# Attention and two MLPs on one core: the second block of queries is taken from the second batch

## The chip, the cores and the metric

The kernel runs on one core of one Trainium2 chip. The metric is the device time of one execution in microseconds (us); lower is better. TensorE is called PE in the profile (its weight loads PEld), VectorE DVE, ScalarE ACT, GpSimd POOL and SyncE SP.

## The reference

A causal attention with a forget gate (4 batches, 8 heads, 576 positions, head size 64) is followed by two MLPs over its 2304 rows of 512 numbers. Everything is float32.

```
scores = q @ k.T / 8 + min(-(cum_i - cum_j), 0)      # cum: running sum of max(s, 0) along the positions
attn   = softmax(causal(scores)) ;  x = attn @ v      # then (batch, position) x (head, size) -> 2304 x 512
h      = x @ w_in1 ;  x2  = (s * relu(h)**2 + b) @ w_out1
h      = x2 @ w_in2;  out = (max(h, 0) + alpha * min(h, 0)) @ w_out2
```

The MLPs treat each row by itself, so the order in which rows go through them is free as long as each result goes to its row of the output.

## The kernel before, in words

**Units of attention.** Work is cut into 32 units. A unit is one batch, one pair of heads and one of two ranges of queries: range 0 is queries 0 to 319, which see keys 0 to 319; range 1 is queries 320 to 575, which see all 576 keys. The list `units` (L210) goes batch by batch, within a batch range by range, within a range over the four pairs. Four units with the same batch and range are called a group here. Per head, range 0 has three blocks of queries (64, 128 and 128 rows that see 64, 192 and 320 keys) and range 1 has two (128 rows each that see 448 and 576 keys).

**A unit's steps.** `load_qk` (L257), `load_v` (L268) and `load_cum` (L283) issue its DMAs on SP's queue. `transpose_qk` (L302) turns q and k with DVE. `scores` (L337), once per head, prepares the gate term on DVE (L362) and the causal mask on POOL (L366, after memsets at L345, L358 and L360), multiplies q and k on PE (L384, or L386 and L387), adds and finds the maximum on DVE (L388), takes exp on ACT (L394) and scales on POOL (L403). `values` (L409), once per head, transposes the probabilities on PE (L434), copies them out of PSUM, multiplies by v (L450) and writes the result into `x_block(t)`, the input tile of MLP block t (L455 to L467).

**Native and split units.** Units 0 to 7 (`NATIVE = 2 * NP`, L54) are native: PE multiplies the float32 tiles as they are, and a listing of PE shows two passes for each product. From unit 8 on each operand is split into a high and a low float32r part (ACT, POOL and DVE work at L106, L107, L326 to L334), and scores and values are each two float32r products; `values` then copies and adds at L465 and L466 in place of the one copy at L463.

**MLP blocks and pace.** The rows are cut into 9 blocks of 256 (T), in the order in which the units produce them, and go through the first MLP block by block while attention runs on, then through the second. A block has 16 steps f, each with `up` (PE at L575; ACT and DVE at L596 to L599; a split at L106 and L107) and `down` (PE at L616, in the second MLP L626), and at its end `finish` (L631), which copies the result out (L637, L639) and stores it. In block 0 of the first MLP each step also converts one packet of weights (`load_packet`, L157: DMA of 1 MB, ACT at L116, DVE at L117 and L118, then a split on ACT and POOL). `reached(t)` (L656) says how many units must be done before block t can be read, and `pace` (L660) how many units are emitted at each step. For t = 0 to 8 it gives 4, 8, 12, 16, 20, 24, 28, 28 and 32 units.

**Order.** The program is emitted in the order of the loop at L679; a planner then orders each engine's instructions by its own estimates and by what is ready. So each engine's list mixes MLP steps, weight packets and attention at fine grain.

**Where the stages lie.** Unit 4, the first of the second group, has its scores on PE from 49.58 us on; DVE's last instruction on a packet of weights (L118) starts at 148.19 us; block 0 of the first MLP is copied out (L639) at 165.97 us and block 1 at 234.35 us. The units of a group follow each other without a gap.

Of the kernel before, what the change touches and what calls it, by code (L numbers as in the profile page):

```python
# [18 lines left out]
def tile_forget_attention__then__two_mlps(  # L19
# [20 lines left out]
    nc = tc.nc  # L40
    B, H, S, D = q.shape
    NT, DM = out.shape
    DFF = w_in1.shape[1] // 2
    P = 128
    NP = H // 2
    NCC = DM // P
    NF = DFF // P
    T = 256
# [3 lines left out]
    R1 = IB[2][1]  # L52
    QK = S - R1 + S
    EARLY, NATIVE = NP, 2 * NP  # L54

# [47 lines left out]
    def split(hi, lo, src, lo_eng=nc.vector):  # L105
        nc.scalar.copy(hi, src)  # L106
        lo_eng.tensor_tensor(out=lo, in0=src, in1=hi.bitcast(F32), op=ALU.subtract)  # L107
# [34 lines left out]
    for f in range(len(SPARE), NF):  # L142
        at = int((f - len(SPARE)) * PACE)
# [50 lines left out]
    def x_block(t):  # L194
        if t not in xf:
            xf[t] = xfp.tile([P, NCC, T], F32, tag="xf", name=f"xf{t}")
        return xf[t]
# [9 lines left out]

    units = [(b, pr, rng) for b in range(B) for rng in range(2) for pr in range(NP)]  # L210
    HALF = (slice(0, 64), slice(64, 128))
    early_bufs = list(range(4 * NF - 2, -1, -2)) + [4 * NF - 1]

# [195 lines left out]
    def values(u, h):  # L409

        own = HALF[h]
        q0, q1, nq = u.q0, u.q1, u.q1 - u.q0

        width = [q1 - max(q0, P * c) for c in range(5) if P * c < q1]
        last_c = len(width) - 1
        banks = ([(0, 0), (1, 320)], [(2, 64)]) if u.rng == 0 else ([(0, 0), (1, 256)], [(2, 0), (3, 256), (4, 448)])
        av = u.bank("av", f"av{h}")
        for n_bank, bank in enumerate(banks):  # L420
            f0, fn = bank[0][1], bank[-1][1] + width[bank[-1][0]]
            tp = u.bank("tr", f"pt{h}_{n_bank}")
            moves = []
            for c, off in bank:
                for r in u.blocks:
                    i0, i1 = IB[r]
                    if P * c >= i1:
                        continue

                    partial = r and P * c > i0  # L430
                    o = off + i0 - max(q0, P * c)
                    moves.append((not partial, -c if partial else o, o, r, min(P * c, S - P)))
            for _, _, o, r, k0 in sorted(moves):
                nc.tensor.transpose(tp[:, o : o + P], u.probs[h][r][:, k0 : k0 + P], ident)  # L434
            n_p = (2 * h + n_bank) % 2
            if u.native:
                pf = two.tile([P, 512], F32, tag=("ph", "pl")[n_p], name=f"pf_{u.tag}_{h}_{n_bank}")
                (nc.scalar.copy, nc.vector.tensor_copy)[n_p](pf[:, f0:fn], tp[:, f0:fn])
                parts = (pf,)
            else:  # L440
                ph = two.tile([P, 512], F32R, tag="ph", name=f"ph_{u.tag}_{h}_{n_bank}")
                pl = two.tile([P, 512], F32R, tag="pl", name=f"pl_{u.tag}_{h}_{n_bank}")
                split(ph[:, f0:fn], pl[:, f0:fn], tp[:, f0:fn])
                parts = (ph, pl)
            yield
            for z, part in enumerate(parts):
                for c, o in bank:
                    w = width[c]
                    lhs = (u.vn if u.native else u.vs[h])[:, c].rearrange("p z d -> p (z d)")
                    nc.tensor.matmul(  # L450
                        av[:, nq - w : nq], lhs, part[:, o : o + w],
                        start=(c == 0 and z == 0), stop=(c == last_c and z == len(parts) - 1),
                        skip_group_check=True,
                    )
        t0 = u.b * S + q0  # L455
        while t0 < u.b * S + q1:
            t = t0 // T
            t1 = min((t + 1) * T, u.b * S + q1)
            a = t0 - u.b * S - q0
            cols = slice(a, a + t1 - t0)  # L460
            dst, src = x_block(t)[own, u.pr, t0 - t * T : t1 - t * T], av[own, cols]
            if u.native:
                nc.scalar.copy(dst, src)  # L463
            else:
                nc.scalar.copy(dst, av[HALF[1 - h], cols])  # L465
                nc.vector.tensor_tensor(out=dst, in0=src, in1=dst, op=ALU.add)  # L466
            t0 = t1  # L467
        yield
# [12 lines left out]
    def attention():  # L481
# [22 lines left out]
        yield from alternate(transpose_qk(us[1]), scores(us[0], 0))  # L504
        yield from alternate(transpose_qk(us[2]), scores(us[0], 1))
        yield from alternate(transpose_qk(us[3]), scores(us[1], 0), values(us[0], 0))
        yield from alternate(scores(us[1], 1), values(us[0], 1))
        yield from alternate(scores(us[2], 0), values(us[1], 0))
        u = Unit(EARLY)
        load_qk(u), load_cum(u), load_v(u)  # L510
# [46 lines left out]
    def mlp_block(layer, t, x):  # L557
# [73 lines left out]
        def finish():  # L631
            both = one.tile([P, 1024], F32, tag="res", name=f"res{layer}_{t}")
            for m in range(2):
                cols = slice(m * 512, (m + 1) * 512)
                res = both[:, cols]
                if m % 2:
                    nc.scalar.mul(res, accs[:, cols], 1.0 / W_SCALE)  # L637
                else:
                    nc.vector.tensor_scalar(  # L639
                        out=res, in0=accs[:, cols], scalar1=1.0 / W_SCALE, scalar2=None, op0=ALU.mult  # L640
                    )
                if layer == 0:
                    nc.sync.dma_start(out=x2_d[t, :, cols], in_=res)
                else:
                    nc.sync.dma_start(out=out[t * T + m * P : t * T + (m + 1) * P, :], in_=res)

        return up, down, finish

# [5 lines left out]
        return packets[layer, f]  # L654

    def reached(t):  # L656
        b, rest = divmod(min((t + 1) * T, NT) - 1, S)
        return NP * (2 * b + (1 if rest < R1 else 2))

    def pace(t):  # L660

        t += LEAD / NF
        n = int(t)
        return reached(n) + (t - n) * (reached(min(n + 1, NB - 1)) - reached(n)) if n < NB else len(units)
# [8 lines left out]
    while done < reached(0):  # L673
        next(side)
# [4 lines left out]
    for n in range(2 * NB * NF):  # L679
# [11 lines left out]
        for j in range(NF):  # L691
            at = LAG[1] + int((j - len(SPARE)) * PACE) if j >= len(SPARE) else j * SPACING - FIRST
# [42 lines left out]
```

## Time and profile before

| | |
|---|---|
| time, median of 3 runs | 1091.94 us (1088.45 to 1092.47) |
| the profiled execution: its time, its span | 1088.58 us, 1086.8 us |
| PE busy, share of the span | 1045.6 us, 96% |
| DVE busy | 666.8 us, 61% |
| ACT busy | 644.4 us, 59% |
| POOL busy | 478.4 us, 44% |

The span is the time from the first to the last instruction; the execution takes 1.8 us more than its span. In the row of PE busy by slices of 27 us, the first slices are the only ones with low digits: `5899999999...`; the granted clock of PE in the same slices is `9699899999...`, in tenths of 2.4 GHz.

### The profile page before, as it was taken

Reading aid. Unit: us, or ns where it says so; the run is one execution under the profiler, and the core shown is the slowest. Engines: PE = TensorE matmul, PEld = TensorE weight load, DVE = VectorE, ACT = ScalarE, POOL = GpSimd, SP = SyncE. Lnnn points to the kernel's source line nnn. Section 1 sums busy time; section 2 is a strip of 40 time slices with the busy share of each in tenths; the row PEclk is TensorE's granted clock in tenths of the full one; section 3 lists DMA queues with packets and bytes.
Section 4 is the critical chain, followed back from the end, with each engine's and each line's share of the span. In section 5 each row is a group of like instructions: output and inputs, shape, how many; then the busy total and the mean of one; then the engine's idle time right before and its main releaser. Section 6 shows DMA issues by size and latency. Waiting matters only on the chain.

```text
span 1086.8 us, 21253 instructions
## 1 busy us (share of the span) xinstructions
PE 1045.6 (96%) x7429; PEld 969.9 (89%) x7429; DVE 666.8 (61%) x1612; ACT 644.4 (59%) x1719; POOL 478.4 (44%) x868
## 2 busy tenths in 40 slices
PE   5899999999999999999999999899999999999998
PEld 3677799999999999999998999789999999999997
DVE  7699878787688877787565167943333333333332
ACT  3686767777767877777565467643444434434332
POOL 6688877665766757666464267820000000000000
PEclk9699899999999999999999999999999999999999
DMA  6987433343232422233134064510100100000000
GB/s 145 236 234 221 136 70 81 80 99 56 50 81 65 109 50 60 67 78 81 34 104 141 12 204 155 175 40 1 40 20 20 40 1 20 2 20 20 2 20 20
DMA packets 170059, 83.85 MB, mean 77 GB/s; under 512 B 135456, under 2 KB 155936, under 8 KB 169952
## 3 DMA queue, kind: packets, MB, share of 16 engines
q1 hardware_dynamic: 168272, 81.94, 28.3%
q8 instruction: 58, 0.95, 0.4%
q10 hardware_dynamic: 1680, 0.57, 0.2%
q14 instruction: 49, 0.40, 0.1%
HBM read 72.96 MB, written 9.51 MB: 76 GB/s over the span
## 4 chain that ended last, share of the span: by engine, by line
PE 67%; DVE 14%; DMA 5%; issue 4%; ACT 4%; POOL 3%; SPq 2%; DVEq 0%; POOLq 0%; ACTq 0%
PE hp L575 29%; PE acc L626 18%; PE acc L616 12%; PE pt L434 3%; DVE probs L362 3%; PE av L450 3%; DMA wo<-in_moe_w_out_dram 2%; DVE probs L388 2%; DVE wt L117 2%; DVE wt L118 2%; SPq L263 1%; DVE r L599 1%; DVE xs L331 1%; PE sc L387 1%; PE sc L386 1%
## 5 line engine op out<-in xcount | busy, mean ns | idle before, releaser
L575 PE MATMUL hp<-xh,w 128*128 128x256 f32 x2304 | 467.5, 285 | 5.6 <-ACT r L596 2.9
L575 PEld LDWEIGHTS hp<-xh,w 128*128 128x128 f32 x2304 | 378.6, 191 | 13.5 <-ACT r L596 4.4
L575 PE MATMUL hp<-xl,w 128*128 128x256 f32 x1152 | 327.2, 284 | 0.0
L575 PEld LDWEIGHTS hp<-xl,w 128*128 128x128 f32 x1152 | 220.3, 191 | 6.3 <-POOL probs L358 0.7
L626 PE MATMUL acc<-w,ring 128*128 128x512 f32 x864 | 220.4, 393 | 1.2 <-POOL ring L107 0.8
L616 PE MATMUL acc<-gh,w 128*128 128x256 f32 x1024 | 201.9, 288 | 5.3 <-ACT gh L106 5.0
L604 DVE SCALAR_TENSOR_TENSOR ring<-ring,nalpha 128x256 f32<-128x256 f32 x144 | 74.6, 520 | 177.3 <-ACT ring L603 176.3
L626 PEld LDWEIGHTS acc<-w,ring 128*128 128x128 f32 x864 | 154.1, 189 | 28.1 <-POOL ring L107 1.2
L616 PEld LDWEIGHTS acc<-gh,w 128*128 128x128 f32 x1024 | 161.1, 191 | 10.7 <-ACT gh L106 7.4
L616 PE MATMUL acc<-gl,w 128*128 128x256 f32 x512 | 149.4, 292 | 2.8 <-POOL gl L107 2.7
L596 ACT ACTIVATE ring<-hp 128x256 f32<-128x256 f32 x144 | 55.5, 385 | 138.6 <-PE hp L575 138.4
L107 POOL TENSOR_TENSOR gl<-r,gh 128x256 fp32r<-128x256 f32 x128 | 99.9, 781 | 63.8 <-ACT gh L106 62.6
L403 POOL TENSOR_SCALAR probs<-probs,sm 64x64 f32<-64x64 f32 (+4 forms) x160 | 93.5, 597 | 61.0 <-DVE sm L400 57.9
L394 ACT ACTIVATE probs<-probs,nm 64x64 f32<-64x64 f32 (+4 forms) x160 | 90.0, 562 | 46.3 <-DVE nm L388 44.9
L599 DVE TENSOR_SCALAR r<-r,gate_s,gate_b 128x256 f32<-128x256 f32 x144 | 80.5, 559 | 58.0 <-ACT r L598 55.8
L106 ACT CAST ring<-ring 128x256 fp32r<-128x256 f32 x144 | 58.5, 407 | 77.3 <-DVE ring L604 65.7
L616 PEld LDWEIGHTS acc<-gl,w 128*128 128x128 f32 x512 | 97.7, 191 | 5.2 <-POOL gl L107 5.1
L107 POOL TENSOR_TENSOR w<-wt,w 128x512 fp32r<-128x512 f32 x63 | 90.4, 1441 | 26.2 <-ACT w L106 22.1
L107 DVE TENSOR_TENSOR ring<-ring,ring 128x256 fp32r<-128x256 f32 x128 | 54.4, 425 | 61.1 <-ACT ring L106 61.1
L434 PE MATMUL pt<-ident,probs 128*128 128x128 f32 x480 | 79.8, 285 | 8.4 <-POOL probs L403 7.8
L388 DVE CUSTOM_DVE_ANT_0 probs<-sc,probs 128x320 f32<-128x320 f32 (+3 forms) x160 | 67.9, 427 | 23.9 <-PE sc L387 18.4
L596 ACT ACTIVATE r<-hp 128x256 f32<-128x256 f32 x144 | 54.6, 379 | 39.3 <-PE hp L575 33.2
(86 smaller groups left out, 1637.2 us busy)
## 6 DMA issues: line engine op xcount, KB each, us to landing
wi<-in_moe_w_in_dram SPq DMA_DIRECT2D x32, 512.0 KB, 4.5
wo<-in_moe_w_out_dram SPq DMA_DIRECT2D x32, 512.0 KB, 5.0
cum<-cum_d SPq DMA_DIRECT2D x32, 288.0 KB, 3.5
cum<-cum_d SPq DMA_DIRECT2D x30, 160.0 KB, 3.1
nat<-in_k_dram SPq DMA_DIRECT2D x64, 72.0 KB, 2.3
x_d<-res SPq DMA_DIRECT2D x18, 256.0 KB, 2.4
x<-x_d SPq DMA_DIRECT2D x9, 512.0 KB, 4.3
out_dram<-res SPq DMA_DIRECT2D x18, 256.0 KB, 2.0
```

Of the source, the lines that this page charges most:

```text
L106: nc.scalar.copy(hi, src)
L107: lo_eng.tensor_tensor(out=lo, in0=src, in1=hi.bitcast(F32), op=ALU.subtract)
L388: nc.vector.tensor_tensor_reduce(out=pt[:rows, j0:j1], in0=scr, in1=pt[:rows, j0:j1], scale=-SCALE, scalar=init, op0=ALU.add, op1=ALU.min, ...
L394: nc.scalar.activation(pt[:rows, :n], pt[:rows, :n], AF.Exp, bias=nm[:rows, m : m + 1], scale=-1.0, accum_out=sm[:rows, m : m + 1],)
L403: nc.gpsimd.tensor_scalar(out=probs[r][:rows, :n], in0=probs[r][:rows, :n], scalar1=sm[:rows, m : m + 1], scalar2=1.0, op0=ALU.mult, op1=A ...
L434: nc.tensor.transpose(tp[:, o : o + P], u.probs[h][r][:, k0 : k0 + P], ident)
L575: nc.tensor.matmul(hs, a[:, c], b[:, c], start=(n == 0), stop=(n == len(terms) * NCC - 1))
L596: nc.scalar.activation(r, hs, AF.Relu, scale=1.0 / W_SCALE)
L599: nc.vector.tensor_scalar(out=r, in0=r, scalar1=gate_s[:, 0:1], scalar2=gate_b[:, 0:1], op0=ALU.mult, op1=ALU.add)
L604: nc.vector.scalar_tensor_tensor(out=r, in0=u, scalar=nalpha[:, f : f + 1], in1=r, op0=ALU.mult, op1=ALU.add)
L616: nc.tensor.matmul(acc[:, d], a[:, d * P : (d + 1) * P], b, start=(f == 0 and d % 2 == 0 and n == 0), stop=(f == NF - 1), skip_group_check ...
L626: nc.tensor.matmul(accs[:, m * DM : (m + 1) * DM], a[:, m * P : (m + 1) * P], b, start=(f == 0 and b is woh and a is gh), stop=(f == NF - ...
```

## The change

The groups get an order of their own. The first two are now range 0 of batch 0 and range 0 of batch 1, the next two range 1 of both; the groups of batches 2 and 3 keep their places. `PLACES` holds for each group where its rows lie in the order of the MLP blocks, its first row in the output, and its count of rows. `values` takes the place from there, the output is stored in pieces that follow the groups, and `reached` reads the same table; it gives the same nine numbers as before.

So units 4 to 7, which are native, become range 0 instead of range 1; units 8 to 11, which are split, become range 1 instead of range 0. The other 24 units stay as they are.

```diff
--- before.py
+++ after.py
@@ -52,6 +52,12 @@
     R1 = IB[2][1]
     QK = S - R1 + S
     EARLY, NATIVE = NP, 2 * NP
+    GROUPS = [(0, 0), (1, 0), (0, 1), (1, 1)] + [(b, rng) for b in range(2, B) for rng in range(2)]
+
+    PLACES = []
+    for b, rng in GROUPS:
+        at = PLACES[-1][0] + PLACES[-1][2] if PLACES else 0
+        PLACES.append((at, b * S + R1 * rng, (R1, S - R1)[rng]))
 
 
 
@@ -207,7 +213,9 @@
 
 
 
-    units = [(b, pr, rng) for b in range(B) for rng in range(2) for pr in range(NP)]
+
+
+    units = [(b, pr, rng) for b, rng in GROUPS for pr in range(NP)]
     HALF = (slice(0, 64), slice(64, 128))
     early_bufs = list(range(4 * NF - 2, -1, -2)) + [4 * NF - 1]
 
@@ -452,11 +460,11 @@
                         start=(c == 0 and z == 0), stop=(c == last_c and z == len(parts) - 1),
                         skip_group_check=True,
                     )
-        t0 = u.b * S + q0
-        while t0 < u.b * S + q1:
+        first = t0 = PLACES[u.n // NP][0]
+        while t0 < first + nq:
             t = t0 // T
-            t1 = min((t + 1) * T, u.b * S + q1)
-            a = t0 - u.b * S - q0
+            t1 = min((t + 1) * T, first + nq)
+            a = t0 - first
             cols = slice(a, a + t1 - t0)
             dst, src = x_block(t)[own, u.pr, t0 - t * T : t1 - t * T], av[own, cols]
             if u.native:
@@ -642,7 +650,11 @@
                 if layer == 0:
                     nc.sync.dma_start(out=x2_d[t, :, cols], in_=res)
                 else:
-                    nc.sync.dma_start(out=out[t * T + m * P : t * T + (m + 1) * P, :], in_=res)
+                    p0 = t * T + m * P
+                    for at, row, n in PLACES:
+                        a, e = max(at, p0), min(at + n, p0 + P)
+                        if a < e:
+                            nc.sync.dma_start(out=out[row + a - at : row + e - at, :], in_=res[a - p0 : e - p0])
 
         return up, down, finish
 
@@ -654,8 +666,7 @@
         return packets[layer, f]
 
     def reached(t):
-        b, rest = divmod(min((t + 1) * T, NT) - 1, S)
-        return NP * (2 * b + (1 if rest < R1 else 2))
+        return NP * next(n + 1 for n, (at, _, m) in enumerate(PLACES) if min((t + 1) * T, NT) <= at + m)
 
     def pace(t):
```

## Rows read from the trace of the kernel before

**Rows 1.** windows: stretch, its us, busy PE, PEld, DVE, ACT, POOL, clock, DMA, GB/s

```profile
54.00:147.00 93.00, 86.45 (x515) 71.97 (x516) 84.78 (x172) 67.71 (x161) 76.53 (x99) 0.93 0.67 181
...
166.00:234.40 68.40, 66.86 (x548) 65.65 (x548) 56.81 (x159) 51.96 (x145) 44.50 (x101) 1.00 0.37 80
```

**Rows 2.** the chain of waits, 54 to 147 us, shares by line

```profile
by line: issue 16.3%; DVE wt L118 9.6%; DVE wt L117 8.6%; DVE probs L362 8.3%; DMA wo<-in_moe_w_out_dram 6.3%; DVE probs L388 5.8%; DMA vn<-in_v_dram 4.7%; DMA cum<-cum_d 4.1%; DVE pf L438 4.0%; DVE r L599 3.8%; POOL probs L403 3.7%; SPq L2
```

**Rows 3.** groups by form, DVE, 54 to 147 us: busy us, mean ns, idle

```profile
L117 DVE TENSOR_SCALAR wt<-wt 128x512 uint32<-128x512 uint32 x25 | 17.8, 713 | 2.0 <-ACT wt L116 2.0
...
L438 DVE COPY pf<-pt 128x512 f32<-128x512 f32 x8 | 5.4, 676 | 0.0
L362 DVE TENSOR_SCALAR probs<-cum,cumT 128x576 f32<-128x576 f32 x6 | 5.1, 848 | 0.0
...
L388 DVE CUSTOM_DVE_ANT_0 probs<-sc,probs 128x448 f32<-128x448 f32 x7 | 4.3, 611 | 0.4 <-PE sc L384 0.4
L388 DVE CUSTOM_DVE_ANT_0 probs<-sc,probs,nm 128x256 f32<-128x256 f32 x8 | 3.7, 460 | 0.3 <-DVE nm L388 0.3
L362 DVE TENSOR_SCALAR probs<-cum,cumT 128x448 f32<-128x448 f32 x6 | 3.7, 611 | 0.0
...
L362 DVE TENSOR_SCALAR probs<-cum,cumT 64x64 f32<-64x64 f32 x2 | 0.8, 424 | 0.0
L362 DVE TENSOR_SCALAR probs<-cum,cumT 128x320 f32<-128x320 f32 x2 | 0.7, 371 | 0.0
L362 DVE TENSOR_SCALAR probs<-cum,cumT 128x192 f32<-128x192 f32 x2 | 0.6, 302 | 0.0
...
L117 DVE TENSOR_SCALAR last<-last 128x512 uint32<-128x512 uint32 x1 | 0.4, 408 | 0.0
L388 DVE CUSTOM_DVE_ANT_0 probs<-sc,probs 64x64 f32<-64x64 f32 x2 | 0.4, 192 | 0.0
L388 DVE CUSTOM_DVE_ANT_0 probs<-sc,probs 128x192 f32<-128x192 f32 x1 | 0.3, 344 | 0.0
L438 DVE COPY pf<-pt 128x64 f32<-128x64 f32 x1 | 0.2, 216 | 0.0
```

**Rows 4.** groups by form, POOL, 54 to 147 us

```profile
L403 POOL TENSOR_SCALAR probs<-probs,sm 128x576 f32<-128x576 f32 x8 | 8.5, 1068 | 0.0
...
L403 POOL TENSOR_SCALAR probs<-probs,sm 128x448 f32<-128x448 f32 x8 | 6.0, 754 | 4.0 <-DVE sm L400 3.2 <-DMA cum<-cum_d 0.7
...
L358 POOL MEMSET probs<- 128x64 f32 x12 | 1.7, 153 | 0.7 <-PE pt L434 0.6
L366 POOL TENSOR_SCALAR_AFFINE_SELECT probs<-probs 64x64 f32<-64x64 f32 x2 | 0.9, 466 | 1.0 <-DVE probs L362 1.0
...
L403 POOL TENSOR_SCALAR probs<-probs,sm 128x320 f32<-128x320 f32 x1 | 0.5, 528 | 0.0
L403 POOL TENSOR_SCALAR probs<-probs,sm 128x192 f32<-128x192 f32 x1 | 0.4, 420 | 0.0
...
L403 POOL TENSOR_SCALAR probs<-probs,sm 64x64 f32<-64x64 f32 x1 | 0.3, 312 | 1.2 <-DVE sm L400 1.2
```

**Rows 5.** timeline of PE; start us, duration us, merged count

```profile
28.26 1.13 PE L384 MATMUL sc<-turnedk,turnedq 64*128 64x192 f32 x6
...
49.58 1.99 PE L384 MATMUL sc<-turned 64*128 64x448 f32 x6 [0.31 <-DVE turned L308]
51.49 1.30 PE L450 MATMUL av<-pf,vn 128*128 128x320 f32 x6
...
91.78 1.95 PE L450 MATMUL av<-pf,vn 128*128 128x256 f32 x10
...
95.82 1.04 PE L434 MATMUL pt<-ident,probs 128*128 128x128 f32 x8
```

**Rows 6.** the chain of waits in order of time; start us, us

```profile
162.65 1.44 PE hp L575 x12
```

**Rows 7.** DMA issues, whole span; KB each, median us to landing

```profile
out_dram<-res SPq DMA_DIRECT2D x18, 256.0 KB, 2.0
```

## The prediction

> **What bounds the kernel now.** I read the busy shares first: PE 96%, so for most of the span only PE's work and PE's gaps count. Then the windows, to see where that is not so. From 166 to 234.4 us, an ordinary block of the first MLP with attention beside it, PE is busy 66.86 of 68.40 us at full clock, and it stands idle for 1.54 us [rows 1]; there, more PE work is more time. From 54 to 147 us, where block 0, its weight packets and units 4 to 7 lie, PE is busy 86.45 of 93.0 us, but at a mean granted clock of 0.93 (partly at the lower level, 1.2 GHz), DVE 84.78 us and POOL 76.53 us [rows 1]. Three engines are close to full, so the windows alone don't name the bound. The chain of waits over the same stretch does: six DVE lines (L118, L117, L362, L388, L438, L599) have 9.6 + 8.6 + 8.3 + 5.8 + 4.0 + 3.8 = 40.1% of it, POOL shows 3.7% and no PE line is among the first eleven [rows 2]. So the dense stretch is paced by DVE, and all after it by PE.
>
> **What the change moves.** The same 32 units are computed; only which ones are native changes. Units 4 to 7 (8 heads, in the dense stretch) turn from 2 blocks of 448 and 576 keys into 3 blocks of 64, 192 and 320; units 8 to 11 (8 heads, from about 147 us on) turn the other way.
>
> *Dense stretch, DVE.* Per head, L362 goes from 0.848 + 0.611 to 0.424 + 0.302 + 0.371 us, 0.362 less. L388 loses pieces of 448 and 256 columns (0.611 + 0.460) and gains 64 and 192 (0.192 + 0.344), 0.535 less; a piece of 320 is in both. The second copy of L438 falls from 512 columns to 64, 0.676 to 0.216, 0.460 less [rows 3]. Together 1.357 us a head, 10.9 us for 8.
>
> *Dense stretch, POOL.* L403 goes from 1.068 + 0.754 to 0.528 + 0.420 + 0.312, 0.562 less. One more mask (0.466) and four more memsets (five at L345, L358 and L360 in place of one, at 0.153) add 1.078 [rows 4]. That is 0.516 more a head, 4.1 us for 8; the four memsets of v for native range 1 go (0.6), so POOL gains 3.5 us. The memsets need nothing but a free buffer; but behind them in POOL's list stand the masks, which L388 waits for.
>
> *Dense stretch, PE.* Per head, six score passes take 1.13 us for range 0 and 1.99 for range 1; values 1.30 for six passes and 1.95 for ten; three of nine transposes fall away, at 1.04 / 8 = 0.13 [rows 5]. That is 0.86 + 0.65 + 0.39 = 1.90 us, 15.2 us for 8. PE does not pace this stretch, so I count none of it; it is cover.
>
> *Dense stretch, ACT and queues.* ACT keeps its large copies and has three exps in place of two; it is busy 67.71 of 93.0 us [rows 1], nothing. SP issues the same eight DMAs of q and k and two of the gate sums for each unit, all shorter, and one fewer for v; units 8 to 11 take that one over. Less is moved in the stretch where DMA is busiest (0.67 of the engines [rows 1]); I count nothing for it, and up to a microsecond of gain is open, since waits for v and the gate sums have 4.7 and 4.1% of the chain [rows 2].
>
> *How far the stretch shrinks.* The trace has no run with these units here, so this is bounded. If DVE alone paces it, it shrinks by 10.9 us. If DVE and POOL act as one resource, their 84.78 + 76.53 = 161.31 us of busy time fall by 10.9 - 3.5 = 7.4, and the stretch by 93.0 x 7.4 / 161.31 = 4.3 us. The chain is nearly all DVE's, so I take a value nearer the upper end, 9.0 us.
>
> A row that speaks for the lower end: the same DVE shift of 128x512 words takes 713 ns in the mean of 25 and 408 ns once, at the end of the packets [rows 3]; DVE's busy time here holds waiting that isn't its own work. The Trainium skill (SBUF — State Buffer, Who interferes with whom) says that VectorE and GpSimd share one pair of ports as an exclusive lock, so that the later one stops for the whole of the other's instruction. The trace agrees with that as far as 713 against 408 ns goes. By that rule POOL's added 3.5 us would be felt by DVE, and the sum would be that of the lower end, which has its own chance below.
>
> *The price later.* Per split head, scores and values are two products each, over 1024 + 1024 columns for range 1 and 576 + 576 for range 0: 1792 columns more. Twelve products of 256 columns take 1.44 us, 0.469 ns a column [rows 6], so 0.84 us, and with three transposes (0.39) 1.23 us a head, 9.8 us for 8. Here PE is the bound, so this is time, except what fits into its idle time: 1.54 us in a stretch of this kind [rows 1]. Price between 9.8 and 8.3 us. I take 8.3, because the price spreads over more than one stretch and heavier attention gives PE more to choose from. DVE, POOL and ACT get more split work here, but are busy 56.81, 44.50 and 51.96 of 68.40 us; that cover has 11.6 us on DVE.
>
> *The output.* Group borders at rows 320, 1472 and 1728 cut three stores in two, so 21 DMAs in place of 18, at about 2.0 us each [rows 7]. They lie in the second MLP, where the next block's `up` alone, 16 steps of 1.44 us [rows 6], is 23 us long before the result buffer is needed again: nothing. The last block is not cut, so the end of the kernel is not touched. Added waits: none beyond those of the buffers.
>
> **Sum.** -9.0 + 8.3 = -0.7 us. The profiled execution of 1088.58 us (span 1086.8 and 1.8 around it) becomes 1087.9. It was the fastest of what is shown; on the median of 1091.94 us the same step gives 1091.2 us.
>
> **Rivals.**
> 1. *DVE and POOL as one resource.* The stretch shrinks by 4.3, the sum is +4.0, 1095.9 us. For it: 713 against 408 ns. Against it: POOL has 3.7% of the chain.
> 2. *Faster: the lower clock goes too.* With DVE ahead, PE gets its products without gaps. The stretch now loses 0.07 x 93.0 = 6.5 us of full clock; if half to all of that returns beside DVE's 10.9, it shrinks by 14.1 to 17.4, and the sum is -5.8 to -9.1; I set it at -7.5, 1084.4 us. For it: DVE's share of the chain, and 15.2 us less for PE. Against it: a PE with less to do in a stretch that others pace waits more, not less.
> 3. *Slower: POOL takes DVE's place.* At 76.53 + 3.5 = 80.0 us, POOL would be busy 95% of 84 us. If its extra masks and memsets stand in front of what L388 and the scaling of L403 need, all 3.5 us come off the joint 4.3 and the stretch shrinks by 0.8 us: +7.5, 1099.4 us. It decides for slower by half a per cent once the stretch shrinks by less than 2.8 us. For it: POOL is 82% busy. Against it: on the chain its L403 gets shorter, not longer.
> 4. *The weights set the end of the stretch*, and attention is hidden behind them anyway: the shrink is nothing and the sum +8.3, 1100.2 us. For it: L117 and L118 lead the chain. Against it: L362, L388 and L438 stand on the same engine in between, with 18% of the chain.
>
> **How the numbers follow.** A measurement of this kernel tells about 0.5%, 5.5 us, from no change: below 1086.5 us is faster, above 1097.4 slower. Chances: forecast 0.40 (shrink 4.3 to 10.9, price 8.3 to 9.8: 1089.3 to 1097.4), rival 1 0.14, rival 2 0.26, rival 3 0.15, rival 4 0.05. Forecast and rival 1 are no change, 0.54; faster 0.26; slower 0.20. The range takes in the forecast's own, three fifths of rival 2 and half of rival 3, from 1083.0 to 1099.5 us.
>
> **What would show it.** In the profile after: native scores of units 4 to 7 on PE with 64, 192 and 320 columns, and the start of DVE's last instruction on weights (now at 148.19 us) some 9 us earlier. If it is 4 us earlier or less and POOL's lines have gained on the chain, rival 1 or 3 holds; if it is over 13 us earlier and the clock of the stretch is above 0.93, rival 2. If block 0 starts its copy-out 9 us earlier and block 3 or 4 does so by about a microsecond, the price is as I put it; if the lead is kept past block 2, the price was wrong. From 600 us on the two profiles should run in parallel.

## The result and the profile after

The changed kernel takes 1106.39 us (median of 4 runs, 1105.12 to 1107.6) against 1092.2 us for the kernel before in the same session: the ratio is 1.0143, 95% interval 1.0126 to 1.0159, or 14 to 17 us slower. The prediction was 1091.2 us with a range to 1099.5: wrong, and wrong in sign where it mattered, since the stretch that was to shrink by 9 us did not shrink at all.

The windows of the changed kernel: the dense stretch as in [rows 1], the rest of block 0, then blocks 1 and 2 up to their copy-outs (columns as in [rows 1]).

```profile
54.00:147.00 93.00, 80.23 (x461) 65.44 (x461) 79.76 (x158) 61.87 (x163) 72.19 (x120) 0.87 0.61 169
147.00:168.20 21.20, 17.76 (x125) 16.61 (x124) 14.29 (x35) 13.48 (x33) 12.28 (x20) 0.92 0.45 87
168.20:241.40 73.20, 69.72 (x564) 67.70 (x563) 60.61 (x146) 53.23 (x128) 46.10 (x76) 1.00 0.36 79
241.40:315.70 74.30, 73.54 (x599) 72.83 (x599) 56.38 (x159) 54.25 (x142) 47.92 (x95) 0.98 0.30 67
```

Between 54 and 147 us every engine is now less busy than in [rows 1]: PE by 6.2, DVE by 5.0, ACT by 5.8, POOL by 4.3 us, and the clock is lower, 0.87. Yet the stretch is not shorter. The copy-out of the blocks (first and last start in the row) moves from 165.97 to 168.2 us for block 0, and the later ones, worked out from the traces, are late by 7.0 us (block 1), 12.7 (block 2), 12.0 (block 4), 20.8 (block 6) and 19.3 (block 8); from there on the profiles run in parallel. The profiled executions took 1107.6 us here and 1088.58 us before, so their distance of 19 us is some 5 us more than that of the medians.

```profile
L647 DVE TENSOR_SCALAR res<-acc x18: 670/692/693, 168.2 to 1101.4; 128x512 f32<-128x512 f32 x18
```

DVE by form, 54 to 147 us, to be read beside [rows 3] (L117 is now L123, L362 L370, L388 L396, L438 L446):

```profile
L123 DVE TENSOR_SCALAR wt<-wt 128x512 uint32<-128x512 uint32 x23 | 16.8, 733 | 5.0 <-ACT wt L122 5.0
L124 DVE SCALAR_TENSOR_TENSOR wt<-wo,wt 128x512 uint32<-128x512 uint32 x11 | 14.4, 1313 | 0.2
...
L370 DVE TENSOR_SCALAR probs<-cum,cumT 64x64 f32<-64x64 f32 x6 | 5.1, 849 | 0.0
...
L396 DVE CUSTOM_DVE_ANT_0 probs<-sc,probs 128x320 f32<-128x320 f32 x8 | 3.7, 460 | 0.0
L370 DVE TENSOR_SCALAR probs<-cum,cumT 128x320 f32<-128x320 f32 x6 | 2.8, 463 | 0.0
...
L370 DVE TENSOR_SCALAR probs<-cum,cumT 128x192 f32<-128x192 f32 x6 | 1.9, 323 | 0.0
L446 DVE COPY pf<-pt 128x64 f32<-128x64 f32 x8 | 1.7, 218 | 0.6 <-PE pt L442 0.6
```

POOL by form, the same stretch, beside [rows 4] (L403 is L411):

```profile
L411 POOL TENSOR_SCALAR probs<-probs,sm 128x320 f32<-128x320 f32 x8 | 5.5, 692 | 0.0
L411 POOL TENSOR_SCALAR probs<-probs,sm 128x192 f32<-128x192 f32 x8 | 5.4, 678 | 0.0
...
L411 POOL TENSOR_SCALAR probs<-probs,sm 64x64 f32<-64x64 f32 x8 | 4.8, 596 | 6.3 <-DVE sm L408 4.4 <-DMA nat<-in_k_dram 0.9 <-DVE nm L396 0.6
L366 POOL MEMSET probs<- 128x64 f32 x19 | 3.2, 230 | 3.1 <-PE pt L442 2.8
```

In the mean the small instructions take about twice what the prediction gave them from one or two samples: the gate of 64x64 849 ns and not 424, the scaling of 64x64 596 and not 312. The means hide a spread: three of the six gates take 234 to 237 ns and three 867 to 2009, and the 424 was itself the mean of 614 and 234. Per head L370 is .849 + .323 + .463 = 1.635 us, more than the 1.459 of the two large gates, and L411 is 1.966 where 1.260 was expected.

One DVE instruction at two times shows how large the spread can be (timeline of DVE, changed kernel; start us, duration us), and below it POOL at the first of them:

```profile
74.75 3.81 DVE L607 TENSOR_SCALAR r<-r,gate_s,gate_b 128x256 f32<-128x256 f32 x1
...
81.71 0.40 DVE L607 TENSOR_SCALAR r<-r,gate_s,gate_b 128x256 f32<-128x256 f32 x1
```

```profile
75.19 1.26 POOL L113 TENSOR_TENSOR w<-wt,w 128x512 fp32r<-128x512 f32 x1
76.42 0.71 POOL L113 TENSOR_TENSOR gl<-r,gh 128x256 fp32r<-128x256 f32 x1
77.08 0.09 POOL L353 MEMSET sm<- 128x1 f32 x1
77.14 1.27 POOL L113 TENSOR_TENSOR w<-wt,w 128x512 fp32r<-128x512 f32 x1
```

The same DVE instruction takes 0.40 us at 81.71, where POOL has only short memsets, and 3.81 us when POOL has a train of work: it began under the scaling that precedes the train and ends at 78.56 us, the train at 78.41. No DVE instruction of the kernel before lasts over 2.5 us between 54 and 240 us; in the changed kernel three do. Whether this sets the kernel's time is theory C below.

Last, when the units end. The `sm` instruction of unit 7's second head (L399, now L407) starts at 140.09 us before and here:

```profile
144.34 0.59 DVE L407 TENSOR_SCALAR sm<-sm 128x3 f32<-128x3 f32 x1
```

Units 4, 5, 6 and 7 pass that point at 67.6, 90.4, 114.8 and 140.1 us before, and at 70.0, 103.1, 126.3 and 144.3 us after. The weights went the other way: the first half of the last packet has its last DVE step at 121.98 us instead of 130.95. So the weights ran ahead, and the units, which have some 0.6 of their former PE work, came later. That is already in DVE's order, which the planner fixed before the run: the instruction above stands behind 11 of block 0's `r` steps (L599, now L607) before and behind 13 after, and the same one of unit 5 behind 17 weight steps (L118, now L124) before and 24 after. Block 1 can't start without units 4 to 7, nor block 2 without units 8 to 11. At the start of block 2, PE waits for the input split (timeline of PE):

```profile
239.28 0.38 PE L583 MATMUL hp<-xh,w 128*128 128x256 f32 x1
241.20 0.39 PE L583 MATMUL hp<-xl,w 128*128 128x256 f32 x1 [1.54 <-POOL xl L113]
```

### The profile page after: what moved, and what is told of

The parts are those of the page before. It is cut to its first block, busy times and chain, and to the rows that moved or that the text cites. A ratio compares the mean times of both kernels' runs of the same rounds, so it can differ in the third digit from the quotient of the medians.

```text
span 1105.8 us, 21243 instructions
## 1 busy us (share of the span) xinstructions
PE 1047.0 (95%) x7429; PEld 972.4 (88%) x7429; DVE 680.5 (62%) x1612; ACT 650.0 (59%) x1723; POOL 481.2 (44%) x868
## 4 chain that ended last, share of the span: by engine, by line
PE 69%; DVE 13%; ACT 5%; DMA 5%; issue 4%; SPq 2%; POOL 2%; DVEq 0%; POOLq 0%; ACTq 0%
PE hp L583 30%; PE acc L634 17%; PE acc L624 12%; PE av L458 3%; PE pt L442 3%; DVE probs L370 2%; DVE wt L123 2%; DVE wt L124 2%; DMA wi<-in_moe_w_in_dram 2%; DVE xs L339 1%; DVE r L607 1%; DMA wo<-in_moe_w_out_dram 1%; PE sc L395 1%; PE sc L394 1%; SPq L271 1%
## 5 line engine op out<-in xcount | busy, mean ns | idle before, releaser
L583 PE MATMUL hp<-xh,w 128*128 128x256 f32 x2304 | 476.1, 288 | 13.7 <-ACT r L604 9.0
L583 PEld LDWEIGHTS hp<-xh,w 128*128 128x128 f32 x2304 | 383.8, 194 | 24.4 <-ACT r L604 11.7
L583 PEld LDWEIGHTS hp<-xl,w 128*128 128x128 f32 x1152 | 223.2, 194 | 7.5 <-POOL xl L113 2.5
L624 PE MATMUL acc<-gh,w 128*128 128x256 f32 x1024 | 198.5, 286 | 4.6 <-ACT gh L112 2.8
L411 POOL TENSOR_SCALAR probs<-probs,sm 64x64 f32<-64x64 f32 (+3 forms) x160 | 97.3, 620 | 64.2 <-DVE sm L408 60.3
L607 DVE TENSOR_SCALAR r<-r,gate_s,gate_b 128x256 f32<-128x256 f32 x144 | 77.8, 541 | 61.7 <-ACT r L606 58.9
L402 ACT ACTIVATE probs<-probs,nm 64x64 f32<-64x64 f32 (+3 forms) x160 | 89.8, 562 | 43.1 <-DVE nm L396 41.3
L113 POOL TENSOR_TENSOR w<-wt,w 128x512 fp32r<-128x512 f32 x63 | 87.3, 1391 | 23.3 <-ACT w L112 21.6
L396 DVE CUSTOM_DVE_ANT_0 probs<-sc,probs 64x64 f32<-64x64 f32 (+3 forms) x160 | 67.7, 426 | 21.6 <-PE sc L395 12.9
```

The costliest lines, as they stand in the source:

```text
L396: nc.vector.tensor_tensor_reduce(out=pt[:rows, j0:j1], in0=scr, in1=pt[:rows, j0:j1], scale=-SCALE, scalar=init, op0=ALU.add, op1=ALU.min, ...
L402: nc.scalar.activation(pt[:rows, :n], pt[:rows, :n], AF.Exp, bias=nm[:rows, m : m + 1], scale=-1.0, accum_out=sm[:rows, m : m + 1],)
L411: nc.gpsimd.tensor_scalar(out=probs[r][:rows, :n], in0=probs[r][:rows, :n], scalar1=sm[:rows, m : m + 1], scalar2=1.0, op0=ALU.mult, op1=A ...
L583: nc.tensor.matmul(hs, a[:, c], b[:, c], start=(n == 0), stop=(n == len(terms) * NCC - 1))
L607: nc.vector.tensor_scalar(out=r, in0=r, scalar1=gate_s[:, 0:1], scalar2=gate_b[:, 0:1], op0=ALU.mult, op1=ALU.add)
L624: nc.tensor.matmul(acc[:, d], a[:, d * P : (d + 1) * P], b, start=(f == 0 and d % 2 == 0 and n == 0), stop=(f == NF - 1), skip_group_check ...
```

## The experiments

Letters in the expectations. A: in the planned order the units' loads and steps stand too far behind the weight packets. B: the heavier split units cost their PE work wherever they stand. C: POOL's trains block DVE, so that DVE's saving comes back as blocked time. D: a unit with three blocks per head has more steps from engine to engine, and these set its time. F and F2: shorter products leave PE with gaps, the clock falls, and that slows the units. G: the planned order of units against MLP steps. Ratios are to the kernel before in the same session, with 95% intervals.

**Which part of the change.** One kernel keeps range 1 out of units 8 to 15, so that the dense stretch has the changed units and the heavier units come only at 16 to 19; one leaves the dense stretch as before and only exchanges the two groups behind it.

```diff
-    GROUPS = [(0, 0), (1, 0), (0, 1), (1, 1)] + [(b, rng) for b in range(2, B) for rng in range(2)]
+    GROUPS = [(0, 0), (1, 0), (2, 0), (0, 1), (1, 1), (2, 1), (3, 0), (3, 1)]  # e1_early_only
+    GROUPS = [(0, 0), (0, 1), (1, 1), (1, 0)] + [(b, rng) for b in range(2, B) for rng in range(2)]  # e2_late_only
```

> Groups in the order (batch, range) = (0,0), (1,0), (2,0), (0,1), (1,1), (2,1), (3,0), (3,1): units 4 to 7 become native range 0 as in the change, but units 8 to 11 stay split range 0 as before; the heavier groups come from unit 12 on. In the changed kernel the copy-out of block 0 is 2.2 us late and those of blocks 1 and 2 add 4.8 and 5.7. Theory A (two separate losses: the dense stretch gives nothing because attention is placed behind the weights, and units 8 to 11 of range 1 hold up blocks 1 and 2): block 0 again about 2 us late, blocks 1 and 2 no further loss, in all about 1094 to 1098 us. Theory B (the heavier split units cost their PE work wherever they stand, 8 to 10 us): the same loss, only later, about 1104 to 1107 us.

> Groups in the order (0,0), (0,1), (1,1), (1,0) and then as before: native units as before, only units 8 to 11 and 12 to 15 trade places, so the amount of work of every kind is that of the kernel before. Theory A (holding up blocks 1 and 2): slower than before by 5 to 10 us, 1097 to 1102, all of it by the copy-out of block 2. Theory B (only the amount of PE work counts): 1092 us, within 3 us of before.

The first takes 1101.89 us (1.0093, 1.0056 to 1.0130). That lies between the ranges of A and B. Block 0 to block 2 are copied out 2.1, 1.2 and 5.8 us late, with no heavier unit yet: no shrink. Unit 7 is done at 148.7 us, 8.6 later than before, and still block 1 is hardly late: a late unit 7 alone does not delay block 1 by as much. Then block 3, where units 16 to 19 are heavier, takes 80.7 us in place of 70.0. The window of block 3:

```profile
308.80:389.50 80.70, 77.58 (x625) 76.48 (x625) 65.99 (x165) 58.97 (x143) 47.61 (x84) 0.98 0.35 76
```

PE is busy 77.6 us there against 68.5 in the kernel before: the price of 8.3 to 9.8 us stands, found by itself. The second takes 1097.42 us (1.0055, 1.0030 to 1.0080) though its work is that of the kernel before: the exchange of the two groups costs 3 to 9 us. A had all of it by the copy-out of block 2, but in the profile that is only 1.6 us late and block 8's 7.8 us: the loss lies mostly behind block 2, and what makes it is open.

**Order (A).** Attention that is emitted in block 0 gets a higher rank with the planner, in the changed kernel and in the one before.

```diff
-            next(side, None)
+            with tc.high_priority(300) if n < NF else nullcontext():
+                next(side, None)
```

> The changed kernel, with the instructions of attention emitted during block 0 ranked 300 places ahead for the planner; in its list on SP the loads of unit 7 then stand behind packet 11 of the weights instead of 13, those of unit 8 behind 14 instead of 15. Theory A (attention behind the weights in the planner's lists is what the dense stretch loses): unit 7 is done by 138 us or earlier instead of 144, block 0 is copied out 4 to 8 us earlier, in all 1098 to 1102 us. Rival (three engines or their shared resource are simply full): no change, 1105 to 1107.

> The kernel before with the same rank for attention. Its SP list has the same places of loads and packets as without. Every theory: 1090 to 1094 us; more than 5 us away from before would say that the rank itself, not the place of attention, moves the time.

1101.56 us (1.0098, 1.0071 to 1.0125) and 1092.11 (1.0013, 0.9985 to 1.0041). The rank does what it should: the weights end 9.5 us later than in the changed kernel, and unit 7 stands behind 11 `r` steps in DVE's order, as in the kernel before. The time is some 5 us below the changed kernel's and in A's range, with intervals that don't meet, though from separate sessions. Units 5 and 6 are done at 94.4 and 121.1 us, 8.7 and 5.2 sooner, but unit 7 is not, 145.2 us, and block 0 is copied out 4.7 us later where A wanted it sooner. So A may have a part, by these ratios a third; the larger part of the loss stays with the way cleared.

**POOL and DVE (C).** In units 4 to 7 the scaling goes to ACT, or the memsets to DVE, or both.

```diff
+            if u.native and u.n >= EARLY:
+                nc.scalar.mul(probs[r][:rows, :n], probs[r][:rows, :n], sm[:rows, m : m + 1])
+                continue
...
-            nc.gpsimd.memset(sm[:, 0:1], 1.0)
+            clear.memset(sm[:, 0:1], 1.0)          # nc.vector for native units from EARLY on; the other memsets too
```

> The changed kernel, with the scaling of the probabilities (L411) of units 4 to 7 on ACT in place of POOL; same values, same number of hops. Theory C (POOL's trains block DVE, so DVE's saving came back as blocked time): POOL loses 8 x (0.53 + 0.42 + 0.31) = 10 us between 54 and 147 us, DVE's stretch over its own floor falls from 32.7 to 27 us or less, unit 7 is done by 140 us (144.3 in the changed kernel), and the time is 1096 to 1101 us. Rival D (the added hops between engines set the pace of these units): the hops stay, unit 7 at 143 to 147 us, time 1103 to 1109 us.

> The kernel before, with the scaling of units 4 to 7 (L403) on ACT: POOL loses 8 x (1.07 + 0.75) = 14.6 us between 54 and 147 us. Theory C: DVE's stretch over its floor falls from 25.9 us, and the kernel gets faster, 1084 to 1089 us. Rival D: 1089 to 1093 us, no change; or slower if ACT is the next to fill up (67.7 + 12 of 93 us).

> The changed kernel, with the memsets of units 4 to 7 (L353, L366, L368, some 40 instructions) on DVE in place of POOL; the same number of steps. POOL loses about 6 us, DVE gains 3 to 6 us of work of its own. Theory C in its form 'POOL and DVE are one resource': nearly nothing in total, 1103 to 1108 us. If what blocks DVE is the number of POOL's instructions that start while DVE works: 1100 to 1104 us. Rival D: masks no longer queue behind memsets in POOL's list, but wait for DVE instead: 1104 to 1108 us.

> The changed kernel with both: scaling on ACT, memsets on DVE; POOL keeps masks and splits only. Theory C: as the kernel with the scaling alone, or up to 3 us below it, 1094 to 1101 us; POOL's busy time between 54 and 147 us falls by 16 us to about 56. Rival D: 1103 to 1109 us.

1104.6 us (1.0128, 1.0076 to 1.0179), 1097.63 (1.0056, 1.0032 to 1.0081), 1107.91 (1.0159, 1.0134 to 1.0185) and 1105.6 (1.0137, 1.0103 to 1.0171). The times are as D had them. The fall that C wanted is in none; only its weakest form, in which moving work from POOL to DVE changes nothing, fits the run with the memsets. The dense stretch with the scaling on ACT, in the slowest of its four executions (1111.15 us):

```profile
54.00:147.00 93.00, 78.20 (x413) 63.02 (x414) 70.32 (x151) 66.05 (x174) 65.15 (x97) 0.80 0.57 161
```

DVE is at 70 and POOL at 65 of 93 us; 9 and 7 us less than in the changed kernel, and unit 7 is done at 151.7 us, later than D had it too (143 to 147). Part of that is work that comes too late for the window. POOL relieved of the scaling, of the memsets or of both gives nothing back, so its load doesn't set the time. DVE's own work was lightened in none of these runs; only its busy time fell, and the units came no sooner. In the kernel before, 14.6 us less for POOL gained nothing either; it became some 6 us slower, which had been allowed for if ACT fills up.

**PE's work and clock (F).** Scores and transposes of units 4 to 7 are done twice, into the same place; or, in the kernel before, part of its value products is left out.

```diff
+                    for _ in range(2 if u.n >= EARLY else 1):                                    # likewise the transposes
                         nc.tensor.matmul(all_, u.qk[0][own, aq], u.qk[1][own, j0:j1], start=True, stop=True)
...
+                    if u.native and u.n >= EARLY and c in (1, 2, 3):                             # e11_before_less
+                        continue
```

> The changed kernel with PE filled up again: in units 4 to 7 every score product and every transpose of the probabilities is done twice into the same place (same values; by rows 5 of the kernel before some 8 x (1.13 + 0.78) = 15 us of PE work more at full clock). Theory F (with shorter native products PE has gaps, its clock falls to the lower level for a large part of 54 to 147 us, and its steps then take twice as long): the mean clock of the stretch rises from 0.87 to 0.93 or more, the full-clock time lost there falls from 11.9 to 7 us or less, unit 7 is done no later than in the changed kernel (144.3 us), and the time is 1095 to 1106 us in spite of the added work. Rival D (hops and order set the pace, the clock only follows): the added work lengthens the hops, unit 7 at 145 to 152 us, time 1107 to 1118 us.

> As the run before, with the scaling of units 4 to 7 on ACT too. That kernel without the fill had DVE at 70 and POOL at 65 of 93 us between 54 and 147 us, but a clock of 0.80 and 18.8 us of full clock lost. Theory F: clock 0.92 or more, loss under 8 us, and the time falls from 1104.6 to 1092 to 1101 us. Rival D: 1105 to 1116 us.

> The kernel before, with PE work taken away and nothing else: of the value products of units 4 to 7 those over the key tiles 1, 2 and 3 are left out, 704 of 1088 columns, 1.95 x 0.65 = 1.26 us a head, 10.1 us for 8. Theory F: the mean clock between 54 and 147 us falls under 0.93, the lost full-clock time rises above 6.8 us, and the kernel gets no faster or slower, 1090 to 1100 us. Rival D, and my prediction's reading that PE does not pace this stretch: clock unchanged, 1086 to 1092 us.

> The kernel before with the same fill (scores and transposes of units 4 to 7 twice, some 8 x (1.99 + 1.17) = 25 us of PE work at full clock): what the fill costs where the clock was at 0.93 already. PE is then 86.5 + 25 - 7 of 93 us, so it must become the bound: 1100 to 1112 us by both theories; if the clock rises to 1.00 and the time stays under 1097 us, half of the stretch's loss in the kernel before was clock too (F, strongly).

1106.37 us (1.0140, 1.0102 to 1.0177), 1113.44 (1.0207, 1.0166 to 1.0247), 1092.07 (1.0005, 0.9982 to 1.0027) and 1111.95 (1.0185, 1.0141 to 1.0229). The first falls between the ranges of F and D, the second into D's. The third is inside F's range and at the edge of D's, but the clock of its stretch, 0.94, did not fall as F wanted; the fourth is in the range that both gave. In the changed kernel 15 us more PE work cost nothing in the time; in the kernel before 10 us less gained nothing and 25 us more cost some 20. So that much of PE's work there was cover, as predicted. It was not free where it stood: with the fill, unit 7 is done at 151.5 us and block 0 copied out at 181.09 us, 12.9 later than in the changed kernel, and by block 8 this is made up but for 0.9 us. And in the kernel before with less PE work unit 7 is done at 144.2 us and stands behind 13 `r` steps, both as in the changed kernel, yet nothing is lost. So neither the copy-out of block 0 nor the end of unit 7 tells the kernel's time by itself. The clock did not follow the work. 54 to 81 us, the changed kernel filled, then the kernel before filled:

```profile
54.00:81.00 27.00, 23.23 (x78) 17.70 (x79) 22.49 (x44) 17.09 (x41) 17.83 (x26) 0.50 0.74 209
```

```profile
54.00:81.00 27.00, 23.73 (x127) 17.46 (x126) 25.08 (x45) 17.35 (x38) 18.89 (x21) 0.99 0.91 250
```

PE is equally busy in both, once at 1.2 GHz throughout and once at 2.4. F falls in its form: filling PE up doesn't bring the clock back.

**The gaps and the planned order (F2, G).** 32 products of the identity go into the unused half of `hp` in the first four `up` steps; and LEAD, the steps by which attention is emitted ahead, goes to 6 (changed kernel) or 3 (kernel before).

```diff
+                if layer == 0 and t == 0 and f < 4 and c < NCC - 1:
+                    for _ in range(10 if f == 0 and c == 2 else 2):
+                        nc.tensor.matmul(
+                            hp[:, T : T + P], ident, ident, start=False, stop=False, skip_group_check=True
+                        )
...
-    LAG, AHEAD, LEAD, FIRST, SPACING, PACE = (2, 3), 4, 4, 9, 6, 1.75
+    LAG, AHEAD, LEAD, FIRST, SPACING, PACE = (2, 3), 4, 6, 9, 6, 1.75
```

> The changed kernel with 32 extra products of 128 columns (identity by identity, into the unused half of hp, never read) inside the first four up steps of block 0, ten of them at the place where PE waited 2.48 us at 60.7 us; some 32 x 0.26 = 8.3 us of PE work at full clock. Theory F2 (the low clock between 54 and 81 us, 0.75 in the changed kernel against 0.94 before, comes from PE's gaps there and is what delays units 4 to 7): the clock of 54 to 81 us rises to 0.9 or more, unit 5 is done by 96 us (103.1 in the changed kernel, 90.4 before), time 1096 to 1103 us. If the clock rises and unit 5 and the time don't follow, the clock is a symptom: 1103 to 1110 us. If the clock stays low, the run says nothing of F2.

> The changed kernel with one number changed, LEAD 6 in place of 4: the same work, attention emitted two steps sooner. In PE's planned order the last values of units 9, 10 and 11 then stand behind 21.8, 25.4 and 30.0 up steps in place of 24.4, 29.0 and 32.5 (21.2, 25.3 and 30.0 in the kernel before), and units 28 to 31 stand as in the kernel before. Theory G (the planned order puts units 7 to 11 two to four steps further behind the MLP, so PE waits for them at the starts of blocks 1 and 2, and the tail of the attention gets the dearer of two orders): block 2 starts by 236 us (241.7), blocks 5 to 8 take 247 to 250 us (254.8), time 1094 to 1101 us. Rival D (hops of the three-block units): only what lies behind block 1 can change, 1102 to 1107 us.

> The kernel before with LEAD 3 in place of 4: the same work, but the planned order of units 11 to 31 on PE becomes that of the changed kernel (unit 12 behind 36.0 up steps, units 28 to 31 behind 100, 104, 108 and 113 in place of 100, 106, 110 and 115). Theory G: blocks 5 to 8 take 252 to 256 us in place of 247.5, time 1095 to 1099 us, with no change of work at all. If the order of the tail costs nothing: 1090 to 1093 us.

> The changed kernel with LEAD 6 and the extra products in the first four up steps: if both theories hold, their gains add and it comes to 1090 to 1098 us; if only G holds, as the run with LEAD 6 alone or a little above; if only F2 holds, as the run with the extra products alone.

1100.11 us (1.0091, 1.0059 to 1.0123), 1106.86 (1.0142, 1.0104 to 1.0180), 1093.03 (1.0013, 0.9985 to 1.0041) and 1105.71 (1.0135, 1.0108 to 1.0162). The extra products made the changed kernel some 5 us faster, but in its profile the clock of 54 to 81 us is 0.68 and unit 5 is done at 106.4 us, so this says nothing for F2; why it gained is open, and with LEAD 6 added the gain is gone. LEAD 6 alone brought nothing, and block 2 starts at 248.7 us: G does not explain blocks 0 to 2. LEAD 3 is inconclusive on the tail: in its profiled execution blocks 5 to 8 take 254.2 us as G had it, yet its ratio is worth only 1.4 us (-1.6 to 4.5).

**The third block by itself (D).** The first kernel adds to each head of units 4 to 7 of the kernel before a block of 64 x 64 that nobody reads. The second takes the gate, mask, product, minimum, exp and scaling of the 64-row block out of the changed kernel; its memsets, transposes and values stay, and the first 64 queries of batch 1 get zero probabilities.

```diff
...
+            nc.tensor.matmul(sc[:, :64], u.qk[0][own, :P], u.qk[1][own, :64], start=True, stop=True)  # e17
+            nc.vector.tensor_tensor_reduce(
+                out=extra, in0=sc[:64, :64], in1=extra, scale=-SCALE, scalar=KEEP_ALL,
+                op0=ALU.add, op1=ALU.min, accum_out=nm[:64, 2:3],
+            )
+            nc.scalar.activation(
+                extra, extra, AF.Exp, bias=nm[:64, 2:3], scale=-1.0, accum_out=sm[:64, 2:3]
+            )
...
+            if short and r == 0:  # e18, in each loop over the blocks
+                continue
```

> The kernel before with the suspected cost added by itself: in units 4 to 7 each head gets a third, small block of 64 queries and 64 keys (gate on DVE, mask on POOL, one product on PE, minimum on DVE, exp on ACT, scaling on POOL), whose result nobody reads; group order, large blocks and values stay. By the rows of the kernel before that is 8 x (0.42 + 0.19 + 0.08) = 5.5 us of DVE, 8 x (0.47 + 0.31 + 0.15) = 7.4 us of POOL, some 2 us of PE. Theory D (a third block's steps from engine to engine delay a unit, and units 4 to 7 set the start of block 1): unit 7 is done by 146 us or later (140.1), time 1096 to 1105 us. If the steps cost only their busy time beside other work, as the runs that moved 7 to 15 us of DVE or POOL work would have it: 1090 to 1094 us.

> The changed kernel with the small block's steps left out in units 4 to 7: the first 64 queries of batch 1 get zero probabilities (gate, mask, product, minimum, exp and scaling of 64 x 64 left out; its memsets, transposes and values stay), so each head has two blocks as range 1 had. Theory D: unit 7 is done by 138 us or earlier (144.3), block 2 starts by 236 us, time 1096 to 1101 us, which is the price of the heavier units 8 to 11 alone. If the hops cost nothing: 1103 to 1108 us.

1124.66 us (1.0290, 1.0251 to 1.0329) and 1092.13 us (1.0013, 0.9989 to 1.0037). Adding the block costs 31.6 us; taking it out gives 14 us back, nearly all that the change had lost. Both went beyond what D had said (1096 to 1105 us and 1096 to 1101). Unit 7's second head, first with the block added, then with it removed:

```profile
170.02 0.59 DVE L423 TENSOR_SCALAR sm<-sm 128x3 f32<-128x3 f32 x1
```

```profile
133.65 0.17 DVE L412 TENSOR_SCALAR sm<-sm 128x3 f32<-128x3 f32 x1
```

140.1 us became 170.0 and 144.3 became 133.7. What the added block is itself, from 54 to 171 us, by form:

```profile
L355 POOL TENSOR_SCALAR_AFFINE_SELECT probs<-probs 64x64 f32<-64x64 f32 x6 | 7.3, 1215 | 5.1 <-DVE probs L351 5.0
...
L387 PE MATMUL sc_extra<-turned 64*128 64x64 f32 x14 | 3.8, 360 | 2.2 <-DVE turned L308 2.2
...
L392 ACT ACTIVATE probs<-probs,nm 64x64 f32<-64x64 f32 x7 | 2.4, 345 | 0.0
L432 POOL TENSOR_SCALAR probs<-probs,sm 64x64 f32<-64x64 f32 x7 | 2.2, 312 | 0.0
L351 DVE TENSOR_SCALAR probs<-cum,cumT 64x64 f32<-64x64 f32 x6 | 2.0, 338 | 0.0
...
L388 DVE CUSTOM_DVE_ANT_0 probs<-sc_extra,probs 64x64 f32<-64x64 f32 x7 | 1.5, 212 | 4.1 <-PE sc_extra L387 2.0 <-POOL probs L427 2.0
```

Six to seven of the eight heads lie in this window. Their busy time is 9.5 us on POOL, 3.5 on DVE, 3.8 on PE and 2.4 on ACT; even added up that is 19 us, some 24 for all eight heads, and the kernel lost 32. The dense stretch, with the block added and then with it removed (the profiled execution of the latter took 1097.12 us, 5 over its median):

```profile
54.00:147.00 93.00, 85.59 (x437) 66.66 (x437) 73.64 (x139) 56.20 (x136) 67.90 (x85) 0.81 0.59 168
```

```profile
54.00:147.00 93.00, 80.88 (x459) 68.64 (x460) 78.16 (x155) 65.02 (x162) 75.99 (x115) 0.83 0.68 180
```

No engine of the first is fuller than PE, which is as busy as in [rows 1] but at a clock of 0.81 in place of 0.93; DVE has 11 us more room. The second has unit 7 done 6.5 us earlier than the kernel before at a clock of 0.83: there the low clock doesn't hold the units up.

The pair shows that the third block carries the loss. It does not show by which way, for two other things move with the block. One is the clock. From 54 us to the copy-out of block 0, the kernel before and then the one with the block added:

```profile
54.00:165.97 111.97, 104.53 (x658) 89.35 (x659) 99.48 (x216) 81.07 (x203) 91.85 (x133) 0.94 0.61 163
54.00:190.87 136.87, 124.36 (x663) 99.46 (x663) 96.67 (x208) 78.89 (x198) 90.03 (x139) 0.83 0.48 130
```

The stretch is 24.9 us longer; PE stands idle for 12.5 us of it instead of 7.4, and 17% of 136.9 us at full clock are lost, 23 us, instead of 6% of 112.0, 7 us. Most of the delay in that run stands in the profile as PE at its lower clock. Over 83 executions of the kernel before, recorded beside the experiments, a straight line through time and mean granted clock gives 4.6 us for 0.01; as an estimate, that would put some 4 us of the changed kernel's loss and 6 us of this run's to the clock, whichever is cause and whichever effect. The other is the planned order: unit 7's step stands behind 16 `r` steps with the block added and behind 9 with it removed (11 before, 13 after). The runs on rank and with less PE work speak against the order as the whole cause, but no run changes the block and keeps the order. Which of the block's steps weighs most, and whether its turn in the score banks has a part, was not separated either.

## Why the prediction was wrong, step by step

- *What bounds the kernel now: "the dense stretch is paced by DVE".* This is the step that failed, and with it *how far the stretch shrinks*: 9.0 us were forecast, and block 0 came 2.2 us and unit 7 4.2 us later. DVE's busy time does not give the time: with DVE down to 70 of 93 us (the scaling on ACT) the units came no sooner. What the runs show in its place is that the third block of each head carries the loss: without its steps the changed kernel takes 1092.13 us, 14 less, and the kernel before with such a block added takes 1124.66, 32 more, although its busy time over all engines is some 24 us. The prediction counted the added memsets and masks as POOL's busy time and said "Added waits: none beyond those of the buffers". A reading that fits, but is not shown: what ends last is each unit's own path through DVE, POOL, PE, ACT and back, in queues shared with weights and MLP; the chain in [rows 2] names DVE most often because every unit passes DVE several times, and a third block is one more such path. How much of it is the path, how much the planned order and how much PE's clock stays open.
- *DVE's and POOL's terms.* L388 and L438 came as worked out (0.53 and 0.46 us less a head by the rows of after). L362 was to save 0.36 and costs 0.18 more; L403 was to save 0.56 and costs 0.14 more. Both came from one or two samples of small shapes. That leaves 6.5 of DVE's 10.9 us and turns POOL's 3.5 into 3.5 + 5.6 = 9.1 us by the same sum. Rival 3 had the sign and the place right (POOL), but not the size, 1099.4 us, nor the cause: with POOL relieved nothing came back.
- *PE in the dense stretch, not counted.* Right for the time: 15 us more of it cost nothing in the changed kernel. What PE was spared went into waiting and a lower clock, as was said against rival 2: from 54 us to the copy-out of block 0 it is idle for 16.2 us in place of 7.4, at a clock of 0.88 in place of 0.94.
- *The price later, 8.3 us.* Right in size: blocks 1 to 4 take 285.6 us in place of 275.8, 9.8 more, and moved to block 3 it is 10.7 us there. Block 2's waits for its units are part of it, and the run that only exchanges two groups loses 3 to 9 us without any added work, so of the 9.8 us not all need be PE's work; in block 3 of the first experiment 9.1 us are.
- *What would show it.* The native products of 64, 192 and 320 columns are there. DVE's last instruction on weights went from 148.19 to 153.05 us, while the packet work before it was 9 us early: the sign to look at should have been the units, not the weights.
- *"From 600 us on parallel".* Yes: 18.6 us at block 7, 19.3 at block 8, 18.9 at the end. But blocks 5 to 8 lost another 7 us in the profiled execution with the same work in both. The planned order of units 28 to 31 differs there, and the kernel before in that order shows the same loss in its profile but hardly in its median: open.
- *The output in 21 DMAs: nothing.* The second MLP's blocks keep their 45.1 us.

## What to carry to other kernels

Where many engines are 70 to 90% busy and a chain of small steps runs through all of them, do not cost a change by the busy time alone that it takes off the engine that the chain names most: here cutting work into more and smaller pieces made the kernel slower although PE and DVE had less to do by the sum. Count the added steps as well, and where a planner sets the order, look at what it put in front of them. Take durations of small instructions from many samples of the crowded stretch in which they will run; one or two were off by a factor of two in the mean. And before believing that an engine sets a stretch, relieve it alone and see if the time moves.

## What the runs showed of the hardware that was not expected

- A DVE instruction can last as long as a whole train of POOL instructions: 3.81 us for one of 0.40 us, across four of them, with its end 0.15 us behind the train's. The Trainium skill (SBUF — State Buffer, Who interferes with whom) has the later of the two stop for the whole instruction of the other, where DVE runs in a mode that takes both pairs of ports or reads two inputs from SBUF. The rows fit that, and here the wait spans all that followed without a gap as well; no run shows which mode the instruction ran in, or takes the train away.
- The same busy share of PE stood at either level of its clock: 23.23 of 27 us busy at 0.50 (1.2 GHz) and 23.73 of 27 at 0.99 (2.4 GHz), with 78 and 127 matmul instructions in the rows, in two kernels with the same fill.
- Extra PE work can go with a shorter time: some 8.3 us more of it by estimate, 1100.11 us against 1106.39, in separate sessions; with LEAD 6 the same products gained little (1105.71 against 1106.86, in one session).
